# A decode kernel (attention and a small MLP, mixed by a gate): output projection in four column tiles, and the last key group scored ahead of the last value products

## The chip, the cores and the metric

The kernel runs on one core of a Trainium2 chip. Times are device microseconds (us) of one execution. A *span* is the time from the first to the last instruction in the trace of an execution; the *time* is what the device reports for the whole execution.

The engines are called PE (TensorE matmul), PEld (TensorE weight load), DVE (VectorE), ACT (ScalarE), POOL (GpSimd) and SP (SyncE, which issues nearly all loads). "L475" is line 475 of the kernel.

## The reference, cut to what matters

```python
# B = 8 sequences, one query token each, D = 448, 16 query heads, 8 key/value heads, head size 256.
# The last W = 1024 positions of the caches are used.
q = (x @ wq) in heads;  k, v = last 1024 keys and values, each shared by 2 query heads
p = softmax(q . k * 256**-0.5)
a = (p . v, heads side by side: 4096 values) @ wo              # wo: 4096 x 448
b = gelu(layernorm(x) @ w1 + b1) @ w2 + b2                     # 448 -> 1792 -> 448
g = sigmoid(sum(x * gate_w))
out = g * a + (1 - g) * b                                      # 8 x 448, bfloat16
```

Everything is bfloat16. Keys and values are 33.5 MB each, the weights 11 MB, and each byte is used once.

## The kernel before

The work is cut into `NQ = 16` groups `u` of one sequence and four key/value heads. All large loads go through one ring of 19 slots of 1 MB, in the order of a plan, all issued by SP. The loads of a group are two pieces of keys and two of values.

```python
add_kv("k", A_k_cache, 0)
# ... then w1, wq, w2 ...
for u in range(1, NQ):
    add_kv("k", A_k_cache, u)
    add_kv("v", A_v_cache, u - 1)
add_kv("v", A_v_cache, NQ - 1)
for q in range(NHQ):                       # wo in four quarters, the last one in three pieces
    for j0, j1 in WO_PARTS[q]:
        add(("wo", q, j0), rows_loader([wo_v[:, q, j0 * D : j1 * D]]))
```

For each group the keys are transposed on PE (`ktp`, copied out to `kt` by DVE and ACT), scored against the queries (`S_ps`: sixteen matmuls of 512 columns that go round four strips of 32 PSUM partitions), exponentiated on ACT (`E`), transposed into weights (`sm`, `ET`) and multiplied with the values (`po`: 64 matmuls with only two moving columns each).

```python
for u in range(1, NQ):
    transpose_keys(u)
    values(u - 1, *weights(u - 1))
    scores(u)
    softmax(u)
values(NQ - 1, *weights(NQ - 1))
# ... the head outputs are regrouped (pp, oP): 32 blocks of 128 rows ...
A_ps = ps_misc.tile([NB, D], F32, tag="misc", name="A_ps")
for q in range(NHQ):
    for j0, j1 in WO_PARTS[q]:
        w = slot("wo", q, j0)
        for j in range(j0, j1):
            nc.tensor.matmul(
                A_ps[:, :],                                       # 8 partitions x 448
                lhsT=oP[:, j, q, :],                              # 128 x 8
                rhs=w[:, (j - j0) * D : (j - j0 + 1) * D],        # 128 x 448
                start=(q == 0 and j == 0),
                stop=(q == NHQ - 1 and j == NJ8 - 1),
            )
nc.vector.scalar_tensor_tensor(res[:], in0=A_ps[:], scalar=g_sb[:], in1=mixb[:],
                               op0=ALU.mult, op1=ALU.add)
nc.sync.dma_start(out_f, res[:])
```

## Time and profile before

| | before |
|---|---|
| time, median of the three executions known at the prediction | 204.73 us (204.66 to 205.67) |
| span of the execution whose trace was kept | 204.5 us |
| time of that same execution | 206.27 us |
| bytes moved by the DMA engines | 78.07 MB |

From the page of the kernel before: the heading, four rows of the 40 equal slices of the span (tenths of busy time for PE, of full clock for PEclk, of busy time for the DMA engines, then GB/s), the row of the instruction fetches (packets, MB, share of the DMA engines' span), the shares of the chain that ended last, and two groups of instructions (out<-in, shapes, count; then busy us and mean ns of one; then the idle time just before them and what ended most of it).

```profile
span 204.5 us, 6049 instructions
...
PE   1898697879797979769797979797978797974793
...
PEclk9996589696969696966969696969696969695569
DMA  5999999999999999999999999999999999999710
GB/s 202 400 424 413 421 407 412 405 405 409 405 412 405 409 409 406 412 405 408 409 406 408 408 410 406 408 409 406 405 409 405 410 405 410 407 414 413 311 40 1
...
q8 instruction: 21, 0.34, 0.7%
...
DMA 64%; PE 19%; DVE 8%; ACT 4%; issue 2%; SPq 2%; ACTq 0%
...
L475 PE MATMUL A_ps<-slot,oP 128*8 128x448 bf16 x32 | 8.7, 449 | 0.6 <-DVE oP L468 0.6
...
L482 DVE SCALAR_TENSOR_TENSOR res<-A_ps,g_sb,mixb 8x448 bf16<-8x448 f32 x1 | 0.7, 670 | 8.8 <-PE A_ps L475 8.8
```

The loads run at 400 GB/s or more from the second slice to the fourth from last, with the DMA row at 9 throughout: the kernel is a stream of loads with work hung on it. Only in the last three slices, about 15 us, do the loads fall away while PE goes on. What can be won is there. The next two fences show that end: the timeline (start, duration, engine, line, what, and in brackets the idle time before it and what ended it), and two stretches of it with the busy us of each engine and the granted clock.

```profile
189.45 1.84 PE L357 MATMUL po<-ET,slot 128*128 128x2 bf16 x64 [0.31 <-DVE ET L342]
...
191.65 0.45 PE L460 MATMUL pp<-oT,ident 128*32 128x64 bf16 x16 [0.36 <-DVE oT L366]
...
192.66 8.72 PE L475 MATMUL A_ps<-slot,oP 128*8 128x448 bf16 x32 [0.57 <-DVE oP L468]
...
201.42 0.67 DVE L482 SCALAR_TENSOR_TENSOR res<-A_ps,g_sb,mixb 8x448 bf16<-8x448 f32 x1 [8.81 <-PE A_ps L475]
202.12 0.31 SPq L490 DMA_DIRECT2D out_dram<-res  x1
```

```profile
core 0: us, PE busy (x) PEld busy (x) DVE busy (x) ACT busy (x) POOL busy (x), PEclk, DMA share, GB/s
192.60:197.80 5.20, 5.14 (x14) 1.79 (x15) 0.01 (x1) 0.00 (x0) 0.00 (x0) 0.50 0.28 107
197.80:201.40 3.60, 3.58 (x19) 1.48 (x17) 0.00 (x0) 0.00 (x0) 0.00 (x0) 1.00 0.00 0
```

The projection does not wait for `wo`: it takes 8.72 us on end, at half clock (373 ns from one matmul to the next) until 197.8 us and then at full clock (189 ns). The completion records in the trace, sixteen to a large load and read here as one from each of the 16 DMA engines, say when each load is complete, that is when the slowest engine has finished its share; at the end of this trace the sixteen lie 5.1 us apart. The last three pieces of `wo` are complete at 195.6, 196.18 and 196.74 us, so 4.7 us of matmul lie behind the last byte.

### The profile page before, as it was taken

How to read it: one execution, taken by the hardware profiler on the slowest of the kernel's cores; microseconds unless marked ns; L12 is line 12 of the kernel's file. 1: busy time of each engine (PE TensorE's matmuls, PEld its weight loads, DVE VectorE, ACT ScalarE, POOL GpSimd, SP SyncE). 2: the span in 40 equal slices, each digit the busy share in tenths (PEclk: the TensorE clock that was granted, in tenths of full speed). 3: DMA queues.
4: the chain of work that ended last, by engine and by line, in shares of the span. 5: the costliest groups of instructions: out<-in, count | busy, mean ns of one | idle time of the engine just before them, and what ended most of it. 6: DMA issues, size and time to landing. Idle time of an engine off the chain costs nothing.

```text
span 204.5 us, 6049 instructions
## 1 busy us (share of the span) xinstructions
PE 166.6 (81%) x2734; PEld 133.1 (65%) x2734; DVE 94.3 (46%) x223; ACT 69.8 (34%) x85; POOL 0.8 (0%) x7
## 2 busy tenths in 40 slices
PE   1898697879797979769797979797978797974793
PEld 1798456566666666649595959595958667672531
DVE  6623046273737373706464646464645363633101
ACT  4330025070707070705261616161615343432000
POOL 1000000000000000000000000000000000000000
PEclk9996589696969696966969696969696969695569
DMA  5999999999999999999999999999999999999710
GB/s 202 400 424 413 421 407 412 405 405 409 405 412 405 409 409 406 412 405 408 409 406 408 408 410 406 408 409 406 405 409 405 410 405 410 407 414 413 311 40 1
DMA packets 19801, 78.07 MB, mean 382 GB/s; under 512 B 1440, under 2 KB 1856, under 8 KB 19392
## 3 DMA queue, kind: packets, MB, share of 16 engines
q1 hardware_dynamic: 19600, 77.68, 94.9%
q8 instruction: 21, 0.34, 0.7%
q10 hardware_dynamic: 176, 0.02, 0.1%
q14 instruction: 4, 0.03, 0.0%
HBM read 77.69 MB, written 0.01 MB: 380 GB/s over the span
## 4 chain that ended last, share of the span: by engine, by line
DMA 64%; PE 19%; DVE 8%; ACT 4%; issue 2%; SPq 2%; ACTq 0%
DMA slot<-in_A_k_cache_dram 29%; DMA slot<-in_A_v_cache_dram 28%; DMA slot<-in_A_wq_dram 7%; PE po L357 6%; PE S_ps L305 5%; PE A_ps L475 4%; DVE nmx L317 4%; DVE kt L270 3%; ACT E L320 2%; PE ktp L264 2%; ACT kt L268 2%; PE sm L340 1%; SPq L115 1%; SPq L96 1%; DVE selr L330 1%
## 5 line engine op out<-in xcount | busy, mean ns | idle before, releaser
L264 PEld LDWEIGHTS <-slot 128*128 128x128 bf16 x1024 | 76.0, 115 | 23.6 <-DMA slot<-in_A_k_cache_dram 16.0
L264 PE MATMUL ktp<-ident,slot 128*128 128x128 bf16 x1024 | 82.3, 250 | 9.6 <-DMA slot<-in_A_k_cache_dram 5.0
L270 DVE COPY kt<-ktp 128x1024 bf16<-128x1024 bf16 x80 | 53.1, 687 | 22.1 <-PE ktp L264 21.1
L268 ACT COPY kt<-ktp 128x1024 bf16<-128x1024 bf16 x48 | 47.8, 1012 | 25.0 <-PE ktp L264 24.9
L320 ACT ACTIVATE E<-S_ps,nmx 128x1024 bf16<-128x1024 f32 x16 | 17.8, 1113 | 84.3 <-DVE nmx L317 84.3
L357 PEld LDWEIGHTS <-slot 128*128 128x128 bf16 x1024 | 30.3, 99 | 9.7 <-issue 6.2
L357 PE MATMUL po<-ET,slot 128*128 128x2 bf16 x1024 | 29.3, 163 | 8.0 <-DVE ET L342 5.0
L317 DVE TENSOR_REDUCE nmx<-S_ps 128x1 f32<-128x1024 f32 x16 | 19.6, 1225 | 19.3 <-PE S_ps L305 19.3
L305 PE MATMUL S_ps<-kt,qw 128*2 128x512 bf16 x256 | 24.3, 516 | 0.4 <-DVE qw L291 0.4
L366 DVE TENSOR_TENSOR oT<-po,rb 128x8 bf16<-128x8 f32 x32 | 4.3, 189 | 32.5 <-PE po L357 32.5
L340 PE MATMUL sm<-selr,ones_f 128*128 128x8 f32 x32 | 6.4, 272 | 6.7 <-DVE selr L330 6.6
L340 PEld LDWEIGHTS sm<-selr,ones_f 128*128 128x128 f32 x32 | 5.0, 195 | 8.2 <-DVE selr L330 7.7
L305 PEld LDWEIGHTS <-qw 128*2 128x2 bf16 x256 | 5.4, 93 | 7.2 <-issue 4.5
L475 PE MATMUL A_ps<-slot,oP 128*8 128x448 bf16 x32 | 8.7, 449 | 0.6 <-DVE oP L468 0.6
L333 PE MATMUL sm<-sel,E 128*128 128x8 bf16 x128 | 5.5, 167 | 2.6 <-ACT E L320 2.6
L342 DVE CAST ET<-sm 128x64 bf16<-128x64 f32 x16 | 3.6, 224 | 8.0 <-PE sm L340 8.0
L333 PEld LDWEIGHTS <-E 128*128 128x128 bf16 x128 | 4.9, 97 | 3.5 <-ACT E L320 3.5
L475 PEld LDWEIGHTS <-oP 128*8 128x8 bf16 x32 | 3.3, 105 | 5.7 <-issue 3.4
L281 PE MATMUL qt<-xT,slot 128*128 128x8 bf16 x128 | 4.0, 168 | 2.3 <-DMA slot<-in_A_wq_dram 1.9
L281 PEld LDWEIGHTS <-slot 128*128 128x128 bf16 x128 | 3.8, 104 | 2.5 <-DMA slot<-in_A_wq_dram 2.2
L482 DVE SCALAR_TENSOR_TENSOR res<-A_ps,g_sb,mixb 8x448 bf16<-8x448 f32 x1 | 0.7, 670 | 8.8 <-PE A_ps L475 8.8
L330 DVE TENSOR_SCALAR selr<-sel,rsum 128x8 f32<-128x8 bf16 x16 | 3.7, 232 | 0.6
(58 smaller groups left out, 39.1 us busy)
## 6 DMA issues: line engine op xcount, KB each, us to landing
slot<-in_A_k_cache_dram SPq DMA_DIRECT2D x32, 1024.0 KB, 18.4
slot<-in_A_v_cache_dram SPq DMA_DIRECT2D x32, 1024.0 KB, 18.4
slot<-in_A_wq_dram SPq DMA_DIRECT2D x3, 1024.0 KB
slot<-in_A_wo_dram SPq DMA_DIRECT2D x3, 896.0 KB, 17.9
slot<-in_B_w_dram SPq DMA_DIRECT2D x1, 1008.0 KB, 16.3
slot<-in_B_w_dram SPq DMA_DIRECT2D x1, 896.0 KB, 9.0
slot<-in_B_w_dram SPq DMA_DIRECT2D x1, 560.0 KB, 15.5
slot<-in_A_wq_dram SPq DMA_DIRECT2D x1, 512.0 KB, 16.5
```

Source lines behind the costliest of these rows:

```text
L264: nc.tensor.transpose(ktp[:, c * P : (c + 1) * P], kn[:, o : o + P], ident[:])
L268: nc.scalar.copy(kt[:, j, :], ktp[:])
L270: nc.vector.tensor_copy(kt[:, j, :], ktp[:])
L281: nc.tensor.matmul(qt[:, k, :], lhsT=w[:, c : c + P], rhs=xT[:, r + half, :], start=(r == 0 and k == 0), stop=(r == NR), skip_group_check= ...
L305: nc.tensor.matmul(S_ps[32 * a : 32 * a + rep, hf * NMM : (hf + 1) * NMM], lhsT=qw[:, j, b, h0 : h0 + rep], rhs=KT[a][:, j, hf * NMM : (hf ...
L317: nc.vector.reduce_max(nmx[:], S_ps[:], axis=AXIS.X, negate=True)
L320: nc.scalar.activation(E[:], S_ps[:], ACT.Exp, bias=nmx[:], scale=1.0, accum_out=rowsum[:])
L330: nc.vector.tensor_scalar_mul(selr[:], sel[:], rsum[:])
L333: nc.tensor.matmul(sm[:, c, :], lhsT=E[:, c * P : (c + 1) * P], rhs=sel[:], start=True, stop=True,)
L340: nc.tensor.matmul(sm[:, NC, :], lhsT=ones_f[:], rhs=selr[:], start=True, stop=True)
L357: nc.tensor.matmul(PO[:, j, rep * a : rep * (a + 1)], lhsT=vn[:, o + j : o + Dh : NJ], rhs=ET[:, c, rep * a : rep * (a + 1)], start=(c == ...
L475: nc.tensor.matmul(A_ps[:, :], lhsT=oP[:, j, q, :], rhs=w[:, (j - j0) * D : (j - j0 + 1) * D], start=(q == 0 and j == 0), stop=(q == NHQ - ...
```

## The change

The intent is to end the kernel with the load stream instead of with PE. The output is cut into four column tiles of 112: each block of `oP` is multiplied with each tile, and the four results go to PSUM partitions 0, 32, 64 and 96, where they are to run side by side on the array. (In the trace of before, sixteen score matmuls of 512 columns on four such strips take 1.03 us at full clock; one after the other, at the projection's 189 ns for 448 columns, they would take about 3.5 us, an estimate.) The gate and the MLP result must then lie in the same layout (`gg_s`, `mixb`), and the result leaves in four small DMAs. Besides, key group 15 is loaded and scored before the values of groups 13 to 15, so that no softmax stands between the last value load and its products.

```diff
-    epool = ctx.enter_context(tc.tile_pool(name="epool", bufs=2))
+    epool = ctx.enter_context(tc.tile_pool(name="epool", bufs=3))
@@ the plan
-    for u in range(1, NQ):
+    for u in range(1, NQ - 1):
         add_kv("k", A_k_cache, u)
-        add_kv("v", A_v_cache, u - 1)
-    add_kv("v", A_v_cache, NQ - 1)
+        if u < NQ - 2:
+            add_kv("v", A_v_cache, u - 1)
+    add_kv("k", A_k_cache, NQ - 1)
+    for u in range(NQ - 3, NQ):
+        add_kv("v", A_v_cache, u)
@@ the last groups (cut)
+    transpose_keys(u + 1)
+    W1 = weights(u)
+    values(u - 1, *W0)
+    scores(u + 1)
+    softmax(u + 1)
+    values(u, *W1)
+    A_ps = ps_misc.tile([P, DQ], F32, tag="misc", name="A_ps")
+    nc.vector.memset(A_ps[:], 0.0)
+    values(u + 1, *weights(u + 1))
@@ the projection
-                nc.tensor.matmul(
-                    A_ps[:, :],
-                    lhsT=oP[:, j, q, :],
-                    rhs=w[:, (j - j0) * D : (j - j0 + 1) * D],
+                for dst, cols in quads(A_ps):
+                    o = (j - j0) * D
+                    nc.tensor.matmul(
+                        dst,
+                        lhsT=oP[:, j, q, :],
+                        rhs=w[:, o + cols.start : o + cols.stop],
@@ the output
-    nc.sync.dma_start(out_f, res[:])
+    for i, (src, cols) in enumerate(quads(res)):
+        eng = nc.sync if i % 2 == 0 else nc.scalar
+        eng.dma_start(out_f[:, cols], src)
```

Cut from this diff: the MLP's second product is tiled in the same way (60 matmuls instead of 14), its bias `b2` enters as a fifth matmul per tile, and the gate is spread over the partitions by one small matmul. All of that happens in the first 30 us.

More of the change, by code (lines that the diff above doesn't have):

```diff
@@ L161 @@
     gw_b = consts.tile([NB, D], BF16)
-    b2_b = consts.tile([NB, D], BF16)
+    b2_r = consts.tile([1, D], BF16)
     b1_sb = consts.tile([P, NF], BF16)
@@ L166 @@
     )
-    nc.scalar.dma_start(
-        b2_b[:], B_b2.rearrange("(o d) -> o d", o=1).to_broadcast([NB, D])
-    )
+    nc.scalar.dma_start(b2_r[:], B_b2.rearrange("(o d) -> o d", o=1))
     nc.scalar.dma_start(b1_sb[:], B_b1.rearrange("(p c) -> p c", c=NF))
@@ L180, with quads @@
     NX = NR + 2
+    DQ = D // QUAD
+    def quads(ps):
+        return [
+            (ps[32 * i : 32 * i + NB, :], slice(i * DQ, (i + 1) * DQ))
+            for i in range(QUAD)
+        ]
     xz = consts.tile([NB, 2, P], BF16)
@@ L189 @@
     oT = consts.tile([P, Hq, NJ, NB], BF16)
-    g_sb = consts.tile([NB, 1], F32)
-    omg = consts.tile([NB, 1], F32)
-    b2o = consts.tile([NB, D], F32)
-    mixb = consts.tile([NB, D], F32)
-    res = consts.tile([NB, D], BF16)
+    gg = consts.tile([NB, 2], F32)
+    spread = consts.tile([NB, QUAD, 32], F32)
+    gg_s = consts.tile([P, 2], F32)
+    ones_r = consts.tile([1, NB], BF16)
+    mixb = consts.tile([P, DQ], F32)
+    res = consts.tile([P, DQ], BF16)
+    nc.vector.memset(spread[:], 0.0)
+    nc.vector.memset(ones_r[:], 1.0)
     def transposed(dst, src, srcz):
@@ L246, in norm_and_gate @@
         nc.scalar.activation(gth[:], gl[:], ACT.Tanh, scale=0.5)
-        nc.vector.tensor_scalar(g_sb[:], gth[:], 0.5, 0.5, op0=ALU.mult, op1=ALU.add)
-        nc.vector.tensor_scalar(omg[:], g_sb[:], -1.0, 1.0, op0=ALU.mult, op1=ALU.add)
-        nc.vector.tensor_scalar_mul(b2o[:], b2_b[:], omg[:])
+        nc.vector.tensor_scalar(
+            gg[:, 0:1], gth[:], 0.5, 0.5, op0=ALU.mult, op1=ALU.add
+        )
+        nc.vector.tensor_scalar(
+            gg[:, 1:2], gth[:], -0.5, 0.5, op0=ALU.mult, op1=ALU.add
+        )
+        nc.vector.tensor_copy(
+            spread[:, :, 0:NB],
+            ident[0:NB, 0:NB]
+            .rearrange("p (o b) -> p o b", o=1)
+            .to_broadcast([NB, QUAD, NB]),
+        )
+        gp = ps_misc.tile([P, 2], F32, tag="misc", name="gp")
+        nc.tensor.matmul(
+            gp[:],
+            lhsT=spread[:].rearrange("p i b -> p (i b)"),
+            rhs=gg[:],
+            start=True,
+            stop=True,
+        )
+        nc.vector.tensor_copy(gg_s[:], gp[:])
     KT = {}
@@ L421, in mlp_out @@
     def mlp_out(hs):
-        bb = ps_misc.tile([NB, D], F32, tag="misc", name="bb")
+        bb = ps_misc.tile([P, DQ], F32, tag="misc", name="bb")
+        nc.vector.memset(bb[:], 0.0)
         for c in range(NF):
             w, o = (slot("w2", 0), c) if c < W2A else (slot("w2", 1), c - W2A)
-            nc.tensor.matmul(
-                bb[:, :],
-                lhsT=hs[:, c, :],
-                rhs=w[:, o * D : (o + 1) * D],
-                start=(c == 0),
-                stop=(c == NF - 1),
+            for dst, cols in quads(bb):
+                nc.tensor.matmul(
+                    dst,
+                    lhsT=hs[:, c, :],
+                    rhs=w[:, o * D + cols.start : o * D + cols.stop],
+                    start=(c == 0),
+                    stop=False,
+                )
+        for dst, cols in quads(bb):
+            nc.tensor.matmul(
+                dst, lhsT=ones_r[:], rhs=b2_r[:, cols], start=False, stop=True
             )
         done(2)
-        nc.vector.scalar_tensor_tensor(
-            mixb[:],
-            in0=bb[:],
-            scalar=omg[:],
-            in1=b2o[:],
-            op0=ALU.mult,
-            op1=ALU.add,
-        )
+        nc.vector.tensor_scalar_mul(mixb[:], bb[:], gg_s[:, 1:2])
     norm_and_gate()
@@ L448 @@
     mlp_out(hs)
-    for u in range(1, NQ):
+    for u in range(1, NQ - 2):
         transpose_keys(u)
@@ L453 @@
         softmax(u)
-    values(NQ - 1, *weights(NQ - 1))
+    u = NQ - 2
+    transpose_keys(u)
+    W0 = weights(u - 1)
+    scores(u)
+    softmax(u)
+    transpose_keys(u + 1)
[7 more added lines that the diff above has]
+    values(u + 1, *weights(u + 1))
     pp = ps_sm.tile([P, HPQ, NJ, NHQ, NB], F32, tag="sm", name="pp")
@@ L468 @@
     nc.vector.tensor_copy(oP[:], pp[:].rearrange("p m j q b -> p (m j) q b"))
-    A_ps = ps_misc.tile([NB, D], F32, tag="misc", name="A_ps")
     for q in range(NHQ):
@@ L474 @@
             for j in range(j0, j1):
-                nc.tensor.matmul(
-                    A_ps[:, :],
-                    lhsT=oP[:, j, q, :],
-                    rhs=w[:, (j - j0) * D : (j - j0 + 1) * D],
-                    start=(q == 0 and j == 0),
-                    stop=(q == NHQ - 1 and j == NJ8 - 1),
-                )
+                for dst, cols in quads(A_ps):
+                    o = (j - j0) * D
+                    nc.tensor.matmul(
+                        dst,
+                        lhsT=oP[:, j, q, :],
+                        rhs=w[:, o + cols.start : o + cols.stop],
+                        start=(q == 0 and j == 0),
+                        stop=(q == NHQ - 1 and j == NJ8 - 1),
+                    )
     nc.vector.scalar_tensor_tensor(
@@ L484 @@
         in0=A_ps[:],
-        scalar=g_sb[:],
+        scalar=gg_s[:, 0:1],
         in1=mixb[:],
```

## The prediction

> **What bounds the kernel.** The loads. The page gives 78.07 MB over a 204.5 us span; from 5 us to 190 us every slice of its DMA row is at 9 tenths, 400 to 424 GB/s, and the chain of waits is 64% DMA. The K and V consumers start about 0.04 us after a landing, so reordering equal transfers cannot speed the stream. Only the tail can be won.
>
> By the landing records, the last V piece is complete at 187.97 us, the wo pieces at 190.14, 192.32, 194.52, 195.6, 196.2 and 196.74 us (the 16 engines finish up to 5 us apart; the slowest counts). In the timeline the last value products start at 189.45 (after the last softmax), the output projection at 192.66. Its 32 matmuls of 448 columns take 8.72 us, at granted clock 0.5 until 197.8 (373 ns each, then about 190 ns), and end at 201.40. So 4.7 us of matmul lie after the last wo byte. Then 0.67 us on DVE, 1.3 us from output issue to landing, 1.1 us of closing.
>
> **What the change does.**
> 1. Output projection in column tiles. [...] 16 score matmuls of 512 columns on four column strips take 1.65 us, four at a time at half clock. Four of 112 columns should cost 448/4 columns, about 93 ns at half clock, or four issues at 29 ns (64 value products in 1.84 us), 115 ns. So 32 groups take at most about 3.7 us (estimate), less than the 6.6 us over which wo lands. The projection then waits for wo, and only the last 8 matmuls (about 0.45 us) remain after the last landing.
> 2. DVE result 128x112 instead of 8x448: 0.67 to about 0.3 us (other 128x112 operations here: 0.22 to 0.28).
> 3. Four small output DMAs on two queues: the second on each leaves 0.35 to 0.6 us later, so it costs about 0.4 us. [...]
> 4. K15 ahead of V13 to V15: the last products can end near 189 us instead of 191.3. With tiling the projection waits for wo anyway: about 0. Alone: 1 to 2 us.
> 5. mlp_out in 60 small matmuls, gate spread, smaller b2 load: early, hidden under the DMA stream; 0. About 290 more PE instructions mean one or two more 16 KB instruction fetches, each holding one DMA engine 1.1 us, probably not the slowest.
>
> **Sum.** Last wo landing 196.7; projection done 197.2; DVE 197.55; last output landing 199.3; end 200.4 of span, plus 0.2 between the profiled span and the timed median: 200.6 us, 2.0% below before. On the threshold. Range 199.4 to 202.0; chances 0.50 faster, 0.48 within 2%, 0.02 slower.
>
> **What would show it.** Right: last wo landing again at 196 to 197.5; A_ps matmuls starting near 190 to 191, idle before them ended by wo DMAs, in three or more bursts; A_ps to DVE gap under 0.7 us; DVE near 0.3 us; span ending 3.2 to 3.7 us after the last wo landing. Wrong: A_ps groups of four taking over 250 ns (tiles not concurrent), or a last wo landing that moved.
>
> **What would make it wrong.** The stream ending earlier or later by over 1 us (another engine slowest, a fetch on it); slow small output writes.

The "one or two more" fetches are an estimate; they agree with the page of before, where 5468 PE instructions (matmuls and weight loads) come with 21 fetches, 260 to each.

## The result, and the profile after

The change measured 202.37 us (202.25 to 202.5, four executions) against 205.2 us for the kernel before (204.66 to 205.73, four executions). The ratio is 0.9862, with a 95% interval from 0.9827 to 0.9897: 1.4% faster, inside the 2% band.

From the page of the kernel after, the lines that answer to those of before:

```profile
span 200.4 us, 6333 instructions
...
PEclk9997558888888878797958995899579997996555
DMA  5999999999999999999999999999999999999960
GB/s 195 410 423 411 409 408 406 410 405 410 407 406 410 409 406 410 406 413 405 408 407 407 410 405 410 406 410 409 403 410 407 407 408 409 409 409 411 411 251 21
...
q8 instruction: 22, 0.36, 0.7%
...
DMA 91%; PE 6%; issue 0%; SPq 0%; DVE 0%
...
L518 PE MATMUL A_ps<-slot,oP 128*8 128x112 bf16 x128 | 4.0, 291 | 3.3 <-DMA slot<-in_A_wo_dram 2.5
...
L525 DVE SCALAR_TENSOR_TENSOR res<-A_ps,gg_s,mixb 128x112 bf16<-128x112 f32 x1 | 0.3, 334 | 6.9 <-PE A_ps L518 6.9
```

The chain that ended last is now 91% DMA. The timeline of the end of the kernel after:

```profile
190.49 0.92 PE L518 MATMUL A_ps<-slot,oP 128*8 128x112 bf16 x32 [0.57 <-DVE oP L510]
192.45 0.92 PE L518 MATMUL A_ps<-slot,oP 128*8 128x112 bf16 x32 [1.05 <-DMA slot<-in_A_wo_dram]
...
194.63 0.92 PE L518 MATMUL A_ps<-slot,oP 128*8 128x112 bf16 x32 [1.26 <-DMA slot<-in_A_wo_dram]
...
195.74 1.49 PE L518 MATMUL A_ps<-slot,oP 128*8 128x112 bf16 x32 [0.19 <-DMA slot<-in_A_wo_dram]
...
197.28 0.33 DVE L525 SCALAR_TENSOR_TENSOR res<-A_ps,gg_s,mixb 128x112 bf16<-128x112 f32 x1 [6.85 <-PE A_ps L518]
197.65 0.67 SPq L535 DMA_DIRECT2D out_dram<-res  x2
197.65 0.65 ACTq L535 DMA_DIRECT2D out_dram<-res  x2
```

The projection comes in bursts, and the idle time before each later burst is ended by a `wo` load. A quarter of `wo` is worked off in 0.92 us instead of about 3.0 us at half clock (8 x 373 ns), and the clock was at half throughout. So far the prediction reads like the trace:

| step | predicted, us | this trace, us |
|---|---|---|
| last `wo` landing | 196.7 | 196.83 |
| projection done (DVE starts) | 197.2 | 197.28 |
| DVE done | 197.55 | 197.61 |
| last output landing | 199.3 | 199.49 |
| end of span | 200.4 | 200.4 |
| time | 200.6 | 202.37 (this execution 202.25) |

Each step of the span is right within 0.2 us, and the time is wrong by 1.8 us. The predicted range, 199.4 to 202.0, misses.

### The profile page after: what moved, and what is told of

It is laid out like the page before. It is cut to its first block, busy times and chain, and to the rows that moved or that the text cites. A ratio compares the mean times of both kernels' runs of the same rounds, so it can differ in the third digit from the quotient of the medians.

```text
span 200.4 us, 6333 instructions
## 1 busy us (share of the span) xinstructions
PE 158.8 (79%) x2878; PEld 130.8 (65%) x2878; DVE 93.5 (47%) x228; ACT 70.1 (35%) x85; POOL 0.8 (0%) x7
## 4 chain that ended last, share of the span: by engine, by line
DMA 91%; PE 6%; issue 0%; SPq 0%; DVE 0%
DMA slot<-in_A_v_cache_dram 47%; DMA slot<-in_A_k_cache_dram 30%; DMA slot<-in_A_wq_dram 8%; DMA slot<-in_A_wo_dram 7%; PE S_ps L335 3%; PE po L387 2%; PE ktp L294 1%; PE A_ps L518 0%; SPq L162 0%; DVE res L525 0%; SPq L115 0%
## 5 line engine op out<-in xcount | busy, mean ns | idle before, releaser
L294 PEld LDWEIGHTS <-slot 128*128 128x128 bf16 x1024 | 73.5, 113 | 24.0 <-DMA slot<-in_A_k_cache_dram 15.4
L294 PE MATMUL ktp<-ident,slot 128*128 128x128 bf16 x1024 | 80.2, 246 | 9.4 <-DMA slot<-in_A_k_cache_dram 4.3
L387 PEld LDWEIGHTS <-slot 128*128 128x128 bf16 x1024 | 30.3, 99 | 12.2 <-issue 6.3
L387 PE MATMUL po<-ET,slot 128*128 128x2 bf16 x1024 | 30.3, 164 | 9.7 <-DMA slot<-in_A_v_cache_dram 4.5
L335 PE MATMUL S_ps<-kt,qw 128*2 128x512 bf16 x256 | 23.6, 504 | 0.4 <-DVE qw L321 0.4
L518 PE MATMUL A_ps<-slot,oP 128*8 128x112 bf16 x128 | 4.0, 291 | 3.3 <-DMA slot<-in_A_wo_dram 2.5
L311 PEld LDWEIGHTS <-slot 128*128 128x128 bf16 x128 | 3.7, 104 | 1.3 <-DMA slot<-in_A_wq_dram 0.9
```

The costliest lines, as they stand in the source:

```text
L294: nc.tensor.transpose(ktp[:, c * P : (c + 1) * P], kn[:, o : o + P], ident[:])
L311: nc.tensor.matmul(qt[:, k, :], lhsT=w[:, c : c + P], rhs=xT[:, r + half, :], start=(r == 0 and k == 0), stop=(r == NR), skip_group_check= ...
L335: nc.tensor.matmul(S_ps[32 * a : 32 * a + rep, hf * NMM : (hf + 1) * NMM], lhsT=qw[:, j, b, h0 : h0 + rep], rhs=KT[a][:, j, hf * NMM : (hf ...
L387: nc.tensor.matmul(PO[:, j, rep * a : rep * (a + 1)], lhsT=vn[:, o + j : o + Dh : NJ], rhs=ET[:, c, rep * a : rep * (a + 1)], start=(c == ...
L518: nc.tensor.matmul(dst, lhsT=oP[:, j, q, :], rhs=w[:, o + cols.start : o + cols.stop], start=(q == 0 and j == 0), stop=(q == NHQ - 1 and j ...
```

## The experiments

The question is where the missing gain is. The two traces differ by 4.1 us of span, the times by 2.8 us. Theory 1 is that time minus span is a constant of about 1.8 us, and that the kept trace of the kernel before came from one of its long executions. Theory 2 is that the load stream ends at different moments from one execution to the next. Theory 3 is that the distance between time and span depends on the kernel. Beyond that, the experiments ask which half of the change works, and whether the end of the stream can be moved at all. Twelve runs were made, three of them of the kernel before, unchanged; all gave the reference's result.

### 1. The kernel before, as if it were a change (aa_before, aa_before_2, aa_before_3)

No edit at all. Every execution then lists span, clock and time.

> The kernel before, unchanged, run as if it were a change, so that every execution lists its span and mean granted clock. Theory 1 (the prediction compared a slow execution of before): time minus span is a constant of about 1.8 us in every execution, as in the four of the change (202.25 - 200.4, 202.49 - 200.7), so executions timed at 204.7 us have spans near 202.9, not 204.5, and they are shorter because the TensorE clock came up earlier in the output projection: in a trace with span near 203 the 32 A_ps matmuls take about 7.2 us instead of 8.7. Theory 2 (the stream varies): the shorter executions have an earlier last wo landing. Theory 3 (the offset differs by kernel): spans here are 204.5 at a time of 204.7.

> The kernel before again, for one more trace. The TensorE clock changes only at marks 3.41 us apart. Theory: it rises at the first mark whose preceding 3.41 us lie mostly (over about three quarters) in the projection; in the first trace of before that mark is 5.1 us after the projection's start and the 32 matmuls take 8.7 us, in the second 2.8 us and 7.6 us. So here: matmul time = r + (11.9 - r) x 0.51 us for a rise r us after the start, with r between 2.5 and 6, and time minus span 1.7 to 1.9 us.

> As the run beside it: one more trace of the kernel before, matmul time of the projection = r + (11.9 - r) x 0.51 us for a clock rise r us after its start.

Measured: aa_before 204.81 us (204.52 to 206.07, six executions; ratio 0.9982, interval 0.9938 to 1.0027). Its traced execution has a span of 203.1 us and a projection of 7.60 us, where theory 1 expected about 7.2. In aa_before_2 the clock rose 2.3 us after the projection's start, below the 2.5 expected, at a mark with 68% of its 3.41 us in the projection, and not three quarters. (The three quarters were an estimate from two traces: no rise after 50% in before, a rise after 83% in aa_before.)

Together with the executions of the kernel before in all rounds, 41 of them list both numbers. Time minus span lies between 1.73 and 1.91 us in every one, with a mean of 1.81. For the four of the change it is 1.75 to 1.90. Theory 3 falls, and the first half of theory 1 stands.

The 41 spans fall into two groups with nothing between: 22 from 202.6 to 203.4 us and 19 from 203.9 to 204.9. The kept trace of before, 204.5, is in the upper group; the three executions that the prediction quoted, 204.66 to 205.67, minus 1.8, are spans of about 202.9 to 203.9.

What makes an execution long? From aa_before_2 (span 202.7 us), the timeline's line of the projection and two stretches around it:

```profile
192.26 7.35 PE L475 MATMUL A_ps<-slot,oP 128*8 128x448 bf16 x32 [0.57 <-DVE oP L468]
```

```profile
core 0: us, PE busy (x) PEld busy (x) DVE busy (x) ACT busy (x) POOL busy (x), PEclk, DMA share, GB/s
...
191.20:194.60 3.40, 2.79 (x23) 1.16 (x24) 0.42 (x1) 0.00 (x0) 0.00 (x0) 0.50 0.61 237
194.60:199.60 5.00, 5.00 (x27) 2.09 (x24) 0.00 (x0) 0.00 (x0) 0.00 (x0) 1.00 0.09 35
```

The 32 matmuls are the same as before, but the clock came up at 194.6 us instead of 197.8, so they took 7.35 us instead of 8.72. That is 1.37 us of the 1.8 us between the two spans; the other 0.4 us is the projection's earlier start. The last `wo` landing does not explain it: 196.64 us here, 196.74 in the long one, and both before the projection's end. Theory 2 falls for these two.

In the clock records of these traces the clock is 0.5 or 1.0, and every change in a trace lies a multiple of 3.41 us from the others (33 changes in before and 23 in the change, to within 1 ns of multiples of 3413.3 ns). If the clock rises r us after the start of the untiled projection, its time should be r + (11.9 - r) x 0.51 us, where 11.9 us is 32 x 373 ns and 0.51 is 190/373. Six traces have an untiled projection:

| trace | projection starts | clock rises | r | formula | measured |
|---|---|---|---|---|---|
| before | 192.66 | 197.78 | 5.12 | 8.58 | 8.72 |
| aa_before | 192.41 | 195.25 | 2.84 | 7.46 | 7.60 |
| aa_before_2 | 192.26 | 194.59 | 2.33 | 7.21 | 7.35 |
| aa_before_3 | 191.93 | 195.76 | 3.83 | 7.95 | 8.09 |
| order_only (below) | 190.36 | 195.26 | 4.90 | 8.47 | 8.62 |
| warm_before (below) | 193.48 | 195.92 | 2.44 | 7.27 | 7.41 |

The formula lies about 0.14 us below each. So the tail of the kernel before depends on where the clock's marks fall in an execution: in its four traces r goes from 2.33 to 5.12 us, and the projection's time with it from 7.35 to 8.72. It must be added that only one of the four traces of the kernel before is from the upper group. That the whole upper group has the same cause is likely from the gap between the groups, but only this one trace shows it.

### 2. Each half of the change alone (tiles_only, order_only)

tiles_only takes the change and puts back the plan, the loop and the two `E` buffers of before. order_only takes the kernel before and gives it the new plan, loop and three buffers:

```diff
 # tiles_only, against the change
-    tc.tile_pool(name="epool", bufs=3)
+    tc.tile_pool(name="epool", bufs=2)
+    (plan and loop over groups as in the kernel before; A_ps made and cleared before the last values)
 # order_only, against the kernel before
-    tc.tile_pool(name="epool", bufs=2)
+    tc.tile_pool(name="epool", bufs=3)
+    (plan and loop over groups as in the change; the projection untouched)
```

> The change without its new order of key and value groups (old plan and loop, two E buffers). Theory 1: the same time as the whole change within 0.3 us (202.4), because the projection, even if it starts at 192.7 us, runs at about 115 ns for each group of four and has caught up with wo before its last landing at 196.8. Rival: the order is what makes the projection early enough, and this one is 1 us or more slower than the whole change.

> The new order alone, with the old projection (32 matmuls of 448 columns, one output DMA). Theory 1: the projection starts near 190.5 us instead of 192.7 and ends 1 to 2 us earlier than before, so about 203.5 us, with a spread over executions of 1 us or more that follows the granted clock, as in before. Rival: no gain, because the clock is then half for longer.

Measured: tiles_only 202.42 us (202.19 to 202.6; ratio 0.9848, interval 0.9814 to 0.9883), order_only 203.28 us (202.67 to 204.19; ratio 0.9894, interval 0.9855 to 0.9934). Tiles alone give the time of the whole change (202.37). The timeline of tiles_only, its projection:

```profile
192.25 1.66 PE L504 MATMUL A_ps<-slot,oP 128*8 128x112 bf16 x64 [0.57 <-DVE oP L496]
...
194.66 0.92 PE L504 MATMUL A_ps<-slot,oP 128*8 128x112 bf16 x32 [0.75 <-DMA slot<-in_A_wo_dram]
...
195.80 1.47 PE L504 MATMUL A_ps<-slot,oP 128*8 128x112 bf16 x32 [0.21 <-DMA slot<-in_A_wo_dram]
```

It starts 1.8 us later than in the change, does two quarters without a pause, and waits for the third: it has caught up. The new order starts a projection earlier that has nothing left to be early for. Alone, the order does help, because an untiled projection has no slack: order_only's starts at 190.36 us and ends at 198.98. Its spans still spread from 200.9 to 202.4 us, as those of the kernel before do (202.6 to 204.9), while those of tiles_only stay within 200.4 to 200.8. The two gains do not add: with tiles, the projection ends at the last `wo` landing in either order.

### 3. Keeping the clock up by hand (warm_before)

```diff
+    fill(6)                      # 128x512 matmuls into a spare PSUM tile
+    W1 = weights(NQ - 1)
+    fill(2)
+    values(NQ - 1, *W1)
+    fill(1)
     # ... pp ...
+    fill(2)
```

> The kernel before with 11 filler matmuls of 128x512 in the PE idle times of the last group (6 while the last softmax runs, the others around the last value products), so that the clock is full in the projection. Result unchanged. Theory 1: with the clock at full rate the 32 A_ps matmuls take 6.1 to 6.5 us (190 ns each) instead of 7 to 8.7, and the time falls 1 to 2.5 us below before, to 202.5 to 204, with less spread. Rival (the granted clock in the tail does not matter): time as before, or longer by the fillers' own 0.5 to 1 us.

Measured: 205.18 us (204.22 to 206.35), ratio 0.9983 (0.9936 to 1.003). No gain, and as much spread as before: a miss. In its trace the projection is short (7.41 us) but starts at 193.48 us, 0.8 to 1.6 us later than in the four traces of the kernel before. The fillers did run, but in the trace they did not raise the clock; that they would was the assumption. Three stretches of warm_before between the clock's marks:

```profile
185.70:189.10 3.40, 3.04 (x17) 1.30 (x15) 1.36 (x3) 1.21 (x2) 0.00 (x0) 0.50 1.02 422
189.10:192.50 3.40, 3.40 (x84) 2.38 (x83) 0.56 (x4) 0.00 (x0) 0.00 (x0) 0.50 0.90 361
192.50:195.90 3.40, 3.34 (x9) 0.94 (x9) 0.42 (x1) 0.00 (x0) 0.00 (x0) 0.50 0.45 173
```

PE counts as 89% and 100% busy in the first two, and the clock stayed at 0.5; it rose after the third, which is nearly all 448- and 512-column matmuls. The second stretch is mostly value products with two moving columns. So in these two stretches the busy share of PE in the profile is not what the clock followed; what it does follow was not shown. In the kernel before, a rise did not follow a stretch that lay 50% in the projection (1.71 of 3.41 us, up to the mark at 194.37 us of the kept trace), and did follow one that lay 68% in it (2.33 of 3.41 us, aa_before_2). The first stretch above fits in between, though it has no two-column matmuls: by the timeline about 2.2 us of it, 66%, are 512-column fillers, and no rise followed. That is too close to 68% to call a border. As a test of what a full clock from the start is worth, this run is inconclusive, since that never came about.

### 4. Is the end of the stream tied to instruction fetches? (more_fetch)

The prediction said that the change's extra instruction fetches would probably not land on the slowest DMA engine. The profile's q8 row counts those fetches: 16 KB each, 1.02 to 1.11 us long in the kernel before and in the change. In the completion records of the kernel before, the first and the last of the 16 engines to finish a large load are at most 0.8 us apart before the first fetch, 2.0 to 2.1 after the 1st to the 8th, 3.5 to 3.6 after the 9th to the 16th, and 5.0 to 5.2 from the 17th on: a step at the 1st, the 9th and the 17th fetch. The expectation below builds on these steps. Its 25 or 26 fetches are an estimate: at 260 PE instructions to a fetch (21 fetches in before), 832 more are about 3.2 fetches on top of 22. To see what they cost, 416 dummy matmuls were added in PE's idle time:

```diff
     for u in range(1, NQ - 2):
         # ... values, scores ...
         softmax(u)
+        for _ in range(32):
+            nc.tensor.matmul(
+                dm[:], lhsT=ident[:], rhs=ident[:, 0:NB], start=True, stop=True
+            )
```

> The change plus 416 dummy matmuls (8 columns, 32 after each softmax of groups 1 to 13, in PE's idle time), which is 832 more PE instructions[...]. Result unchanged. Theory (the stream's slowest engine is the one that carried most instruction fetches; they go round 8 engines, so the first of them gets its 4th with the 25th fetch): 25 or 26 fetches, the last wo landing 1.2 to 1.6 us later (about 198.2), and the time longer by the same, near 203.8 us. Rival (fetches are hidden or spread): last wo landing unchanged within 0.4 us.

Measured: 203.46 us (203.31 to 204.05), ratio 0.9907 (0.9874 to 0.994), which is 1.1 us above the change (and 0.9 us above sp4 of experiment 6, which ran beside it on the same chip), with 26 fetches instead of 22. The last `wo` landing is at 198.0 us, 1.17 later than in the change, a little below the range expected. The timeline of more_fetch shows where:

```profile
192.53 0.92 PE L523 MATMUL A_ps<-slot,oP 128*8 128x112 bf16 x32 [1.06 <-DMA slot<-in_A_wo_dram]
195.78 0.92 PE L523 MATMUL A_ps<-slot,oP 128*8 128x112 bf16 x32 [2.34 <-DMA slot<-in_A_wo_dram]
```

The second and third quarter of `wo` are complete 3.26 us apart, against 2.18 in the change; the 25th fetch starts at 193.2 us, between the two. PE had the time for the dummy matmuls: the loads ran at 408 GB/s from 60 to 120 us with them, the rate of the change's own slices there. So instructions on PE had a price in DMA time in this kernel: 832 more came with four more fetches and a last landing 1.17 us later. The change's one extra fetch (21 to 22) came with a last landing only 0.09 us later (196.74 to 196.83); by the table below it fell on an engine that had time to spare.

The completion records show it from the other side. Between the first and the last of the 16 engines to finish a load there are 0.4 us at the first K load of the change and 5.0 us at the last piece of `wo`, and the distance grows in steps: 1.5 to 2.0 us after the 1st to the 8th fetch, 3.0 to 3.6 after the 9th to the 16th, 4.6 to 5.1 from the 17th on. Which engine carried which fetch is not in the trace; that the fetches go round 8 of the 16 is inferred from these steps and from the lengths of the fetches, which repeat every eight (in before 1031, 1031, 1087, 1082, 1068, 1107, 1107, 1093 ns, then 1026, 1026, 1087, 1082, 1072, 1106, 1106, 1095). At the last piece of `wo`, eight engines finish within 2.7 us of the earliest in each of three traces. The other eight, counted from the earliest, are these:

| trace | fetches by then | the other eight engines | estimate from the count, if shared out in turn among eight |
|---|---|---|---|
| before | 21 | three at 3.1 to 3.3 us, five at 4.6 to 5.1 | three with 2 fetches, five with 3 |
| the change | 22 | two at 3.2 to 3.3, six at 4.5 to 5.0 | two with 2, six with 3 |
| more_fetch | 25 | seven at 4.7 to 5.3, one at 6.4 | seven with 3, one with 4 |

The counts agree in all three, and the one engine at 6.4 us is the last landing of more_fetch.

### 5. Giving the burdened engines less to load (low8, few_engines, best)

The idea: if the engines without fetches took more of the load, the stream should end sooner. A load of only 8 partitions was taken to use 8 engines, because the output stores, which have 8 partitions, leave eight completion records at their landing (and one about 0.5 us after the issue), where a large load leaves sixteen (in the change, the first output: one at 198.12 us, eight from 198.78 to 198.87). Which engines those eight are was not shown. low8 loads the first half of the last `wo` quarter in 16 such DMAs, issued by ACT:

```diff
+                nc.scalar.dma_start(t[p : p + 8, 0:n], ap[p : p + 8, :])    # 16 times
```

> The change with one wo piece (448 KB) loaded by 16 DMAs of 8 partitions each from the other issuing queue. In the output DMA of 8 partitions only 8 of 16 completions came from engines[...], so such DMAs use half of the engines: those 8 carry 28 KB more each and the others 28 KB less, about 1.05 us at the stream's rate. Theory A (the engines that carry the instruction fetches are the other half): the last wo landing comes about 1 us earlier, time near 201.4. Theory B (they are this half): it comes about 1 us later, near 203.4. Theory C (mixed): later by less than 1 us.

Measured: 238.14 us (237.7 to 238.93), ratio 1.1595. This says nothing about the idea, since ACT itself came to a halt. From its waits:

```profile
ACT E L360 <- DMA slot<-in_A_wo_dram: 49.3, 1, 49.3
```

These 49 us end with the exponential at 199.0 us, and the 16 issues with their waits are in them (177.9 to 199.0 us in the timeline), so that the softmax and all behind it stood still. few_engines puts the small loads on SP, one behind each of the last 16 key and value loads, and starts from tiles_only; best adds the edit of experiment 6. That the small loads fall on engines that carry no fetches was the assumption.

```diff
+    def with_early_piece(load, i):
+        def both(t):
+            load(t)
+            rows = slice(8 * i, 8 * i + 8)
+            nc.sync.dma_start(wo_e[rows, :], wo_v[rows, NHQ - 1, 0 : NE * D])
+        return both
```

> The tiles alone (no new order), with 560 KB of wo (5 of the 8 row blocks of its last quarter) loaded by 16 DMAs of 8 partitions each, one behind each of the last 16 key and value loads on the same queue, instead of by a 128-partition DMA at the end. DMAs of 8 partitions used 8 engines in the output stores. [...] I expect them to be the engines that carry no instruction fetches: 35 KB more on each of those, 35 KB less on the others, 1.3 us at 26 GB/s. Theory A: the 16 engines end closer together (spread 5.0 us down to about 3), the last wo landing near 195.5 us instead of 196.8, time near 201.1 us against 202.4 of the tiles alone. Theory B (the slowest engine is among the 8): the last landing near 198.1, time near 203.7.

> The same with the load of x on the other issuing queue, as in the earlier run of that: 0.4 us below the run beside it, near 200.7 us if theory A holds, which is over 2% below before.

Measured: few_engines 206.94 us (206.37 to 207.8; ratio 1.0086, interval 1.0043 to 1.0128), best 207.08 us (206.03 to 207.37; ratio 1.0079, interval 1.004 to 1.0118). Both are misses, by 5.8 and 6.4 us. The same stretch, first of few_engines, then of tiles_only (the last column is GB/s):

```profile
160.00:185.00 25.00, 20.95 (x329) 17.96 (x326) 12.22 (x28) 8.90 (x11) 0.00 (x0) 0.73 1.03 373
```

```profile
160.00:185.00 25.00, 21.68 (x390) 17.75 (x390) 11.50 (x29) 9.39 (x11) 0.00 (x0) 0.80 1.03 408
```

The 16 small loads lowered the rate of the whole stream from 408 to 373 GB/s, while the engines count as just as busy. A 1 MB value load has a median of 11.9 us from issue to landing in that stretch, against 18.4 in the kernel before, so fewer bytes were in flight (rate times time gives an estimate of 4.4 MB, against 7.5 at 408 GB/s). But the engines did not stand idle: in the DMA records of that stretch a 4 KB packet takes 179 ns on average, against 164 in tiles_only, which is as large as the loss of rate. Why the packets are slower was not tested. The idea of balancing stays open: neither run tested it cleanly.

### 6. The two ends of the program (x_act, sp4)

x_act moves the load of `x` to the other issuing queue, so that the first K load leaves earlier. sp4 issues all four outputs from SP.

```diff
 # x_act
-    nc.sync.dma_start(x_sb[:], xf)
+    nc.scalar.dma_start(x_sb[:], xf)
 # sp4
-        eng = nc.sync if i % 2 == 0 else nc.scalar
+        eng = nc.sync
```

> The change with the 7 KB load of x moved to the other issuing queue, so that the first K load is issued at 0.74 us instead of 1.18. If the stream's start sets its end, as the chain of waits says, every landing and the time move 0.4 us earlier, to about 202.0. Rival: the first bytes are limited by something else, and nothing moves.

> The change with all four output DMAs issued by SyncE. Issues on one queue are 0.34 us apart in the change's trace, so the last leaves 1.0 us after the first instead of 0.34, and the time should be 0.6 to 0.7 us longer, 203.0. Rival (issue from two queues saves nothing at the end): the same as the change.

Measured on one chip: x_act 202.0 us (201.52 to 202.18; ratio 0.9827, interval 0.9794 to 0.9859), sp4 202.52 us (202.26 to 202.96; ratio 0.9857, interval 0.9825 to 0.989).

x_act is the fastest kernel, below both originals; its interval reaches to both sides of 0.98, so whether it is 2% faster than before is unclear. The size is as expected, 0.4 us below the change (and 0.5 below sp4 on the same chip). But it is not as plain in its trace: the earliest engine finishes the last piece 0.4 us sooner (191.38 against 191.81 us), the slowest at the same 196.83. The six spans go from 199.7 to 200.4 us, and the kept trace is one of the longest.

sp4 lost less than expected. In its trace the last output lands 2.25 us after DVE is done, 1.88 in the change: 0.37 us, not 0.6 to 0.7. In time it is 0.15 us, which these runs don't tell from nothing.

## Why the prediction was wrong

**What failed is the last term of the sum:** "end 200.4 of span, plus 0.2 between the profiled span and the timed median: 200.6 us". The 0.2 us was 204.73, the median time, minus 204.5, the span of the kept trace. These belong to different executions. The traced execution had itself taken 206.27 us, which stands in the same result as its span and was not used. Within one execution the distance is 1.8 us (1.73 to 1.91 in 41 executions of the kernel before, 1.75 to 1.90 in those of the change). With that term the same sum gives 200.4 + 1.8 = 202.2 us, against 202.37 measured, and 1.2% below 204.73, clearly within the 2% band, instead of "on the threshold".

**Behind it is a second thing.** The prediction took the traced 8.72 us of projection as the kernel's own number. It is one draw: three other traces of the same kernel have 7.35 to 8.09 us, with the clock rising at other moments. The 4.1 us between the two traces is the gain over a long execution. Over the 41 executions the kernel before has a mean time of 205.34 us, the four of the change 202.37, so the gain is 3.0 us (1.4%).

Point by point:

1. *Column tiles, at most 3.7 us of projection, only the last 8 matmuls behind the last landing*: right. Within a burst, the four tiles of a group start 1 to 8 ns apart and the groups, after the first, follow about 93 ns apart, 448/4 columns at half clock. A quarter takes 0.92 us, and DVE starts 0.45 us after the last landing. tiles_only shows that the tiles are the whole of the gain. One detail of the prediction is off: the groups of score matmuls that take 1.65 us run partly at full clock; those wholly at half clock take 1.87 us in the trace of before.
2. *DVE 0.67 to about 0.3 us*: right, 0.33.
3. *Four output DMAs cost about 0.4 us*: near. From the end of DVE to the last output landing it is 1.31 us before and 1.88 after, so 0.6.
4. *The new order about 0, alone 1 to 2 us*: right about 0 (202.42 without, 202.37 with). Alone it gave 1.1% of the kernel before, about 2 us.
5. *The early part 0, fetches "probably not the slowest" engine*: right, one more fetch and the last landing 0.1 us later. more_fetch shows that this was luck of size: by the count in experiment 4 the 22nd fetch gave a third one to an engine that had two, and four more in all, the 25th among them, went with a time 1.1 us longer.
6. *The range*: it was laid round 200.6 and carries the same error. With 1.8 us in place of 0.2 it would be 201.0 to 203.6, which holds 202.37. What the chances of "faster" left out is how much the kernel before itself varies.

## What to carry to other kernels

Compare a span with a span and a time with a time, and take both from the same execution: a profile is one draw, and its own time stands beside it (1.73 to 1.94 us above the span here, over all executions of all kernels). If the tail of a kernel is a stretch of a few us of matmuls, ask whether that trace caught the clock rising early or late (2.33 or 5.12 us after the start here, 1.37 us of projection, where the whole gain was 3.0), and take the gain from several executions. When a kernel is a load stream as here, look whether two changes that each shorten the tail add: these did not (order alone 203.28 us, tiles alone 202.42, both 202.37). Once PE waited for the last load, a further head start was worth nothing, and what remained was the stream's own end, its slowest engine, where four more instruction fetches went with a last landing 1.17 us later.
